# Half 1's tap rows accumulated in PSUM, parameters transposed by DMA, and a new instruction order, in a gated state-space and routed-expert kernel

## The chip, the cores and the metric

The kernel runs on one core of one Trainium2 chip, and all times are microseconds of that core. A core has five engines with queues of their own: PE (TensorE, matrix products), DVE (VectorE), ACT (ScalarE), POOL (GpSimd) and SP, which here issues loads and stores. Each engine takes the instructions of its queue in order, and waits for others through semaphores. The metric is the device time of one execution; of the kernel before, three executions took 186.1, 186.47 and 186.91 us, so the median is 186.47.

## The reference

The input `x` is one sequence of L = 2048 tokens with D = 512 channels, in bf16. The output mixes two branches with a gate for each token:

```
g = sigmoid((x * gate_w).sum(-1))
out = g * a + (1 - g) * b

a: K[d,l] = Re sum_n C[d,n] * dt[d]*B[d,n] * exp(dt[d]*A[d,n]*l)      (complex, n = 128 states)
   a      = causal convolution of x with K over l (through an FFT) + x * Dskip
b: r   = x @ w_r;  idx = the 2 tokens with the largest r
   y   = ((silu(x[idx] @ w_gate)) * (x[idx] @ w_up)) @ w_down * sigmoid(r[idx])
   b   = x, with y added at rows idx
```

`dt = exp(log_dt)`. The lags `l` are rounded to bf16 in the reference, so K takes the same value at many lags, and needs to be known only at a grid of lags.

## The kernel before, in words

Channels are split into two halves of 256 (`h` = 0, 1), tokens into two blocks of 1024 (`blk` = 0, 1). A helper class `Prog` records every operation with what it reads and writes, works out all waits from this, and emits each engine's queue. The order isn't found by a scheduler: the list `SEQ`, written out in the source, fixes it (a negative number puts an operation that could run on ACT or DVE on DVE). All operations go through helpers such as `TT` (a DVE product or sum), `AC` (an ACT function), `SCL` (a scaling on ACT or DVE), `EV` (an eviction of PSUM on ACT or DVE), so the profile gives the helper's line for them: L402 for `TT`, L414 for `AC`, L418 for `EV`, L422 for `SCL`, L425 for a load or store, L428 for an adding DMA of POOL.

The stages, which overlap:

1. **Parameters.** `A`, `B` and `C` are loaded as they lie, in rows of states, and turned by 24 TensorE transposes into PSUM (L545); `AL` (real part times dt) and `B16` (angles) come of them. `WW` holds the weights C·B·dt. `log_dt` comes on ACT's queue.
2. **Forward transform.** Each of eight jobs (block × frequency tile `ft`) multiplies the 1024 tokens with cosines and sines (`c_fwd`, tiles F0 to F3): eight matmuls per part give the sum of even and odd tokens (`plus`, L764), which is evicted into the spectrum `X`; four more with the doubled odd tokens subtracted (`minus`, L779) give the difference, evicted too. PSUM has three pairs of banks for this (`fw0`, `fw1`, `fw2`). Block 1 also takes spectra of block 0 as inputs.
3. **Routing.** u is also loaded transposed (`XT`, one transposing load of 2 MB on SP, L526) for the router's products; the top two rows are found, gathered, and sent through the FFN (WG, WU, WD). Their scaled result `ZB` is added into `xp`, a copy of x in device memory, by a scatter of POOL (L748); u is later reloaded from `xp` on SP.
4. **Tables of K.** `exps1`, `exps2`: 32 exponentials for the first lag grid (`TP`) and nine for the second (`EB`) for each half, on ACT. `trig`: angles scaled, a sine, a shift of the phase (L598), and a cosine. `tab1` and `tab2` multiply both on DVE. Slots 0 to 8 of the second table (`TQ`) are multiplied by the weights. The rows for slots 9 to 20 are these rows times a base factor (`BN`): for half 0 as four products, two of them kept apart in `EX` and summed in PSUM by the generation; for half 1 as a complex product with its sums on DVE (`cmul`).
5. **Generation of K** (`kgen`): 64 groups of matmuls (L810; L813 for `EX`) make K at the lag grid, in PSUM banks `kg0` to `kg3`, evicted as `KA`; a selection (`KC`, L827) follows.
6. **Spectrum of K** (`kspec`, L849): products of KC with the constant `c_ksp` give `KK`.
7. **Products** (`products`, DVE): complex products of X and KK, for each half and quarter of frequencies, with four sums per half on POOL's adding DMAs (`accum`, L428).
8. **Inverse** (`inverse`, L927; L930 for the edge correction `KX`·`CO`): eight PSUM banks; each is visited twice (`q` = 0, 1). The result times g goes into u by an adding DMA, or, for the last block, by a DVE instruction (L409). u has by then been multiplied by 1 − g (sixteen instructions, L977 on ACT and L978 on DVE). Stores go out on SP and ACT.

Some buffers share space: half 1's TP table with the FFN weights, c_inv (`G`) with part of it.

Of the kernel before, what the change touches and what calls it, by code (L numbers as in the profile page):

```python
# [247 lines left out]
ONPE = []  # L248
# [36 lines left out]
def kspec_mats():  # L285
# [35 lines left out]
    "73 20 18 0 1 2 3 5 4 24 6 23 27 69 51 70 60 47 54 61 53 65 58 59 52 68 28 29 30 45 50 62 49 64 66 57 43 74 41 79 46 67 77 31 -147 -146 -135 -136 -145 "  # L321
    "10 48 -138 13 11 25 -137 78 -148 81 63 76 19 21 22 71 75 12 26 -33 33 34 35 36 7 176 175 9 182 181 17 -175 37 42 -178 178 14 188 16 179 56 -184 184 "
    "185 44 138 -140 -142 142 148 -150 -152 140 143 -158 -157 -155 -156 55 72 187 80 15 84 82 -181 193 194 152 150 -165 -167 158 -160 -162 162 189 191 190 "
    "-168 8 85 90 91 86 87 -196 196 197 160 163 -225 -227 -228 92 93 94 95 96 113 97 165 168 -172 169 172 192 206 98 99 100 -102 186 200 201 225 228 231 "
    "229 38 102 103 104 105 198 213 230 232 242 321 -244 153 106 107 114 108 109 110 -200 244 245 248 246 247 -321 -319 251 207 40 83 39 111 112 118 130 "
    "131 115 116 170 -235 -234 173 235 236 202 204 250 -320 237 238 239 240 311 310 309 308 -120 120 124 121 125 299 203 205 383 249 -259 306 307 -209 209 "
    "241 303 304 305 253 252 254 255 256 259 263 302 301 -89 122 270 290 276 277 280 268 279 271 292 278 291 275 273 274 272 283 298 294 289 267 297 269 "
    "296 281 282 286 287 288 285 284 293 295 210 384 -212 300 218 219 -221 222 221 386 -124 126 127 132 212 89 257 260 265 262 264 261 266 348 352 350 312 "
    "-314 -316 -129 322 -326 326 323 324 -342 327 339 -339 -341 314 -332 -329 -331 -330 223 349 117 214 216 215 385 316 332 317 -336 -334 336 342 -346 346 "
    "343 344 -403 347 -404 -402 -401 334 392 394 337 393 391 395 -397 129 133 356 -358 404 -406 354 351 397 -412 -410 -411 355 406 358 398 388 399 389 407 "  # L330
    "408 -360 412 415 416 413 387 390 414 417 418 420 419 421 422 424 423 427 425 426 433 428 429 434 430 431 432 435 353 360 361 362 363 217 364 365 439 "
    "440 437 438 441 442 443 444 366 369 380 370 453 454 445 446 375 378 373 447 367 436 455 456 457 458 459 460 461 462 463 465 476 477 478 371 -382 449 "
    "474 473 475 -449 486 451 464 466 469 483 450 484 485 505 452 487 488 494 470 479 480 481 482 493 495 496 498 497 499 467 468 471 472 506 507 568 522 "
    "523 508 509 571 510 511 569 570 526 512 513 572 573 527 514 515 516 517 518 519 525 524 520 521 489 490 491 535 537 536 492 538 540 539 528 530 548 "
    "549 529 546 382 531 533 532 578 500 581 582 583 501 579 580 502 503 557 558 559 550 551 552 589 504 560 562 561 379 541 376 547 553 554 555 377 534 "
    "574 575 576 602 600 577 601 588 590 368 556 372 603 591 592 624 374 563 584 585 587 614 616 615 586 611 613 612 604 606 605 617 607 608 609 610 544 "
    "542 593 625 623 565 594 622 545 619 567 564 621 566 543 595 596 597 599 598 629 631 630 626 627 628 639 638 632 633 634 618 620 635 636 637 641 640 "
).split()]

KB = 1024  # L340


def bass_gated_mix__ssm_conv_s4__moe_arch_mod__prompt_kernel(nc, A_u, A_A_re, A_A_im, A_B_re, A_B_im, A_C_re, A_C_im, A_log_dt, A_Dskip,
# [22 lines left out]
    with ExitStack() as es:  # L366
# [190 lines left out]
        def cbc(c):  # L557
            return BP(0, 128, c, (0, 2), (1, D))
# [393 lines left out]
        def stage(n):  # L952
            P.stage = n
# [103 lines left out]
```

## Time and profile before

| what | us |
|---|---|
| median of three executions | 186.47 |
| the profiled execution's own time | 186.91 |
| its span (first to last event of the profile) | 185.1 |
| DVE busy | 154.6 (84%) |
| PE busy | 137.0 (74%) |
| ACT busy | 127.2 (69%) |
| POOL busy | 19.1 (10%) |
| first exponential starts | 9.28 |
| generation of half 1 starts on PE | 115.78 |
| last inverse matmul ends | 177.1 |

The profile is of one execution. Busy time is an average over stages with different limits, and the engines take turns in setting the pace, so the share alone doesn't say what a change is worth. PE's busy time counts overlapping matmuls at their modelled ends. An instruction that stands after another on the same engine can start a little before the end given for it, so steps are best counted from start to start. The granted clock of PE was 0.925 of full speed over the span.

### The profile page before, as it was taken

What the parts mean: (1) busy time and instruction counts of PE and PEld (TensorE: products, weight loads), DVE (VectorE), ACT (ScalarE), POOL (GpSimd) and SP (SyncE); (2) the same over time, 40 slices, a digit from 0 to 9 for tenths busy, and PEclk for the clock granted to TensorE, in tenths of its full rate; (3) what the DMA queues carried; (4) which work ended last, traced back from release to release, by engine and by line L of the source; (5) the groups of instructions that cost most, each with busy time, mean ns of one, the idle gap of its engine ahead of it and who ended that gap; (6) DMA issues with size and microseconds to landing.
All of it is one profiled execution on the core that took longest, in us unless ns stands there. A gap on an engine that the chain in (4) does not pass through costs nothing.

```text
span 185.1 us, 4226 instructions
## 1 busy us (share of the span) xinstructions
PE 137.0 (74%) x1806; PEld 93.5 (51%) x1806; DVE 154.6 (84%) x240; ACT 127.2 (69%) x226; POOL 19.1 (10%) x25
## 2 busy tenths in 40 slices
PE   0238999999999679987218781996632999999920
PEld 0133446444556223856205671964521788888810
DVE  0188699988999999999999999995299989999740
ACT  0399979999999999999975487392620067796100
POOL 3000000000000000000600000113000303066300
PEclk9999999999999969999657999699996599999996
DMA  4999999976509704004140830199950473859997
GB/s 76 314 214 283 247 255 378 411 251 255 202 9 345 273 4 113 4 4 117 35 125 2 307 150 0 32 204 343 240 100 0 80 147 64 166 57 149 152 215 225
DMA packets 28388, 30.28 MB, mean 164 GB/s; under 512 B 13479, under 2 KB 22962, under 8 KB 28210
## 3 DMA queue, kind: packets, MB, share of 16 engines
q1 hardware_dynamic: 21442, 23.36, 41.3%
q0 software_dynamic: 4352, 5.77, 19.5%
q10 hardware_dynamic: 2576, 0.89, 2.3%
q8 instruction: 14, 0.23, 0.5%
q14 instruction: 4, 0.03, 0.1%
HBM read 20.05 MB, written 4.20 MB: 131 GB/s over the span
## 4 chain that ended last, share of the span: by engine, by line
DVE 28%; ACT 28%; PE 22%; DMA 10%; SPq 4%; issue 3%; DVEq 0%
DVE AR L402 21%; PE ps L927 14%; ACT AR L414 13%; DMA AR<-AR 6%; ACT AR L602 5%; ACT AR L598 5%; PE ps L764 5%; SPq L425 4%; PE ps L849 3%; DMA AR<-c_fwd 3%; DVE AR L422 3%; ACT AR L422 2%; ACT AR L418 2%; DVE AR L409 1%; DVE AR L418 1%
## 5 line engine op out<-in xcount | busy, mean ns | idle before, releaser
L402 DVE TENSOR_TENSOR AR<-AR 128x1024 bf16<-128x1024 bf16 (+6 forms) x127 | 113.4, 930 | 8.6 <-DMA AR<-AR 5.2
L418 ACT ACTIVATE AR<-ps 128x1024 bf16<-128x1024 f32 (+3 forms) x40 | 32.3, 839 | 29.6 <-PE ps L849 20.2
L414 ACT ACTIVATE AR<-AR 128x256 bf16<-128x256 f32 (+3 forms) x100 | 40.7, 485 | 4.3 <-DVE AR L402 4.1
L927 PE MATMUL ps<-AR 128*128 128x256 bf16 x256 | 30.1, 277 | 8.1 <-DVE AR L402 8.1
L764 PE MATMUL ps<-AR 128*128 128x512 bf16 x128 | 30.9, 392 | 0.5 <-DMA AR<-c_fwd 0.5
L927 PEld LDWEIGHTS ps<-AR 128*128 128x128 bf16 x256 | 25.2, 99 | 11.8 <-DVE AR L402 5.8
L849 PE MATMUL ps<-AR 128*128 128x256 bf16 x160 | 20.5, 286 | 3.2 <-ACT AR L418 3.2
L428 POOL DMA_DIRECT2D AR<-AR x14 | 14.6, 1134 | 66.0 <-DVE AR L402 32.0
L764 PEld LDWEIGHTS ps<-AR 128*128 128x128 bf16 x128 | 12.7, 101 | 15.9 <-issue 2.3
L810 PE MATMUL ps<-AR 128*64 128x42 bf16 x512 | 15.0, 198 | 6.7 <-DVE AR L402 3.9
L849 PEld LDWEIGHTS ps<-AR 128*128 128x128 bf16 x160 | 16.0, 103 | 7.0 <-ACT AR L418 4.4
L779 PE MATMUL ps<-AR 128*128 128x512 bf16 x64 | 16.7, 398 | 2.8 <-DVE AR L418 2.8
L810 PEld LDWEIGHTS ps<-AR 128*64 128x64 bf16 x512 | 14.5, 124 | 8.0 <-DVE AR L402 4.1
L602 ACT ACTIVATE AR<-AR 128x1024 bf16<-128x1024 int16 (+1 forms) x14 | 14.8, 1067 | 1.3 <-DVE AR L598 1.1
L422 DVE TENSOR_SCALAR AR<-AR 128x256 int32<-128x256 f32 (+3 forms) x49 | 14.9, 346 | 0.8 <-ACT AR L602 0.7
L414 ACT ACTIVATE AR<-ps,AR 128x256 bf16<-128x256 f32 x24 | 10.0, 470 | 4.6 <-PE ps L927 4.4
L418 DVE CAST AR<-ps 128x1024 bf16<-128x1024 f32 (+2 forms) x10 | 10.6, 1073 | 2.1 <-PE ps L764 2.1
L827 PE MATMUL ps<-AR 128*32 128x128 bf16 (+1 forms) x96 | 7.5, 418 | 6.4 <-ACT AR L418 6.4
L779 PEld LDWEIGHTS ps<-AR 128*128 128x128 bf16 x64 | 6.1, 101 | 10.5 <-DVE AR L418 3.3
L748 POOL DMA_INDIRECT xp<-AR x1 | 2.3, 2319 | 87.6 <-DVE AR L406 87.6
L545 PE MATMUL ps<-AR 128*128 128x128 bf16 x24 | 2.9, 312 | 11.4 <-DMA AR<-in_A_A_re_dram 7.4
L977 ACT ACTIVATE AR<-AR 128x512 bf16<-128x512 bf16 x15 | 9.8, 717 | 0.0
(55 smaller groups left out, 111.7 us busy)
## 6 DMA issues: line engine op xcount, KB each, us to landing
AR<-AR POOLq DMA_DIRECT2D x8, 512.0 KB, 6.0
AR<-c_ksp SPq DMA_DIRECT2D x5, 512.0 KB, 4.4
AR<-in_A_u_dram SPq DMA_DIRECT2D x2, 1024.0 KB, 8.5
AR<-c_fwd SPq DMA_DIRECT2D x4, 512.0 KB, 5.6
AR<-xp SPq DMA_DIRECT2D x2, 1024.0 KB, 6.7
AR<-c_inv SPq DMA_DIRECT2D x1, 2048.0 KB, 12.2
AR<-in_B_w_gate_dram SPq DMA_DIRECT2D x1, 1792.0 KB, 11.9
AR<-in_B_w_up_dram SPq DMA_DIRECT2D x2, 896.0 KB, 12.2
```

What stands on the lines that cost most here:

```text
L402: return P.op(DVE, lambda h: h.tensor_tensor(out=o, in0=a, in1=b, op=op), rd, wr, cost=tt_cost(o, a, b), **k)
L414: return P.op(ACT, lambda h: h.activation(out=o, in_=a, func=func, scale=scale, bias=bias), rd, wr, cost=0.185 + nel(o) * 0.833e-3 + (0.09 ...
L418: return P.op((ACT, DVE), (lambda h: h.activation(out=o, in_=a, func=ACTF.Copy), lambda h: h.tensor_copy(o, a)), rd, wr, cost=(0.185 + n * ...
L422: return P.op((ACT, DVE), (lambda h: h.activation(out=o, in_=a, func=ACTF.Copy, scale=c), lambda h: h.tensor_scalar(out=o, in0=a, scalar1= ...
L428: P.op(POOL, lambda h: h.dma_start(o, i, accum_op=ALU.add), rd, wr, cost=1.4, nbytes=nbytes, dma=True, tag="sum")
L602: return x.activation(out=so(2), in_=lo, func=ACTF.Sin, scale=-SC16 if m else SC16, bias=HPI(0, 128, 0, (1, 1)) if m else 0.0)
L764: last = h.matmul(o, F[ft](0, 128, ((par * 4 + st) * 2 + part) * 128, (1, 128)), U(0, 128, (blk * 8 + st * 2 + par) * D, (1, D)), start=(i ...
L779: last = h.matmul(o, F[ft](0, 128, ((4 + st) * 2 + part) * 128, (1, 128)), UN(0, 128, st * D, (1, D)), start=False, stop=(st == 3 and blk ...
L810: last = hh.matmul(pb(64 * ct, 64, (g - b0) * 42, (1, 42)), TP[h][1 - part](0, 128, g * 128 + ct, (2, 64)), TQ[h][1 - part](0, 128, g * 84 ...
L849: last = hh.matmul(pb(0, 128, n * 256, (1, 256)), KPU[u](0, 128, tau * 128, (1, 128)), KC[h](0, 128, jg * 256, (1, 256)), start=(k == 0), ...
L927: last = hh.matmul(pb(0, 128, e * 256, (1, 256)), G(0, 128, ((par * 2 + part) * 4 + ft) * 512 + (2 * t2 + e) * 128, (1, 128)), X(0, 128, h ...
L977: P.op((ACT, DVE), (lambda h, o=o, tb=tb: h.activation(out=o, in_=o, func=ACTF.Copy, scale=SG(0, 128, 48 + tb, (1, 1))), lambda h, o=o, tb ...
```

## The change

The diff has these parts.

- Half 1's tap rows are made like half 0's: four products, two kept in `EX`, and 256 more matmuls in its generation sum them.
- The parameters come through six transposing loads on SP; the TensorE transposes and their copies go.
- u is no longer scaled by 1 − g. Each second visit of the inverse takes two more matmuls with the negative unit matrix, which subtract u in PSUM, and the edge correction moves from the first visit to the second.
- The forward transform has two PSUM pairs in place of three, and its jobs are listed in twos; generation has two banks in place of four; the selection uses the two banks of `misc`; in `kspec` the two parts of a block share one pair.
- Half 1's exponentials for the first grid are recorded beside half 0's; both halves use one `EB` buffer, as they did. The FFN weights WU and the intermediate CM1, CM2 and CMW move to the space of X, and KA of half 0 leaves the space of u.
- Some small copies of the routing are split or added.
- `SEQ` is another list throughout. In it the scaling of ZB stands after half 1's table on DVE (it stood before the tables' end), and with it the scatter and the reload of u; the first products of half 0 are followed by an eviction, two of KA, and CO; F2, F3 and the second half of u are loaded after XT.

```diff
 SEQ = [int(x) for x in (
...
-        CM1 = B("cm1", oG, 4 * KB, F32); CM2 = B("cm2", oG + 4 * KB, 4 * KB, F32); CMW = B("cmw", oG + 8 * KB, 4 * KB, F32)
+        CM1 = B("cm1", oB + 8 * KB, 4 * KB, F32); CM2 = B("cm2", oB + 12 * KB, 4 * KB, F32); CMW = B("cmw", oB + 24 * KB, 4 * KB, F32)
...
-        WU = [B("wu%d" % i, oF + (16 + 7 * i) * KB, 7 * KB) for i in range(2)]
+        WU = [B("wu%d" % i, oB + (8 + 16 * i) * KB, 7 * KB) for i in range(2)]
...
-        KA = [B("ka0", oA, 64 * 84), B("ka1", oE + 15 * KB, 64 * 84)]
+        KA = [B("ka0", oG + 16 * KB, 64 * 84), B("ka1", oE + 15 * KB, 64 * 84)]
...
-        fw2, pu = PB("fw2", 2, None), PB("pu", 3, None)
-        kgp = [PB("kg%d" % i, 2 + i // 2, i % 2) for i in range(4)]
+        kgp = [PB("kg%d" % i, 2, i) for i in range(2)]
...
-            DQ([(PRM(0, 128, i * D, (128, 4), (1, 128)), dr(prm[i], 0, (128, 128), (128 * 128, 4), (1, 128)))], [], [(PRM, i)], 131072)
+            dp[0] -= 1e3
+            P.op(SP, lambda h: h.dma_start_transpose(PRM(0, 128, i * D, (1, D)), dr(prm[i], 0, (128, D), (1, 128))), [], [(PRM, i)], cost=1.25, nbytes=200000, late=1.8, prio=dp[0])
...
-                        last = h.transpose(pt(0, 128, at + k * 128, (1, 128)), PRM(0, 128, i * D + k * 128, (1, 128)), CB(0, 128, 0, (1, 128)))
...
-        TT(f512(AL), f512(DTB), f512(PT0), ALU.mult, [DTB, (PT0.buf, 0)], [AL])
+        TT(f512(AL), f512(DTB), f512(PRM, 0), ALU.mult, [DTB, (PRM, 0)], [AL])
...
-        EV(BP(0, 128, 0, (1, 2 * D)), PT1(0, 128, 2 * D, (1, 2 * D)), [(PT1.buf, 4), (PT1.buf, 5)], [BP])
...
-            if h == 0:
-                SCL(nb(0, 128, 0, (1, 512)), bi(0, 128, 0, (1, 512)), -1.0, [bi], [nb])
+            SCL(nb(0, 128, 0, (1, 512)), bi(0, 128, 0, (1, 512)), -1.0, [bi], [nb])
             for j, s, c, m in ((13, 0, 8, 1), (9, 5, 4, 0)):
...
-                if h == 1:
-                    cmul(h, lambda p: sl(p, j, c), lambda p: sl(p, s, c), lambda p: bv((bi, br)[p]), ks, [bi, br], lambda p: [(tq(p), ("t", j))])
-                    continue
                 TT(sl(1, j, c), sl(1, s, c), bv(br), MUL, ka(1) + [br], [(qr, ("t", j))])
                 TT(sl(0, j, c), sl(0, s, c), bv(br), MUL, ka(0) + [br], [(qi, ("t", j))])
                 TT(xv(1), sl(0, s, c), bv(nb), MUL, ka(0) + [nb], [(EX[h][1], j)])
                 TT(xv(0), sl(1, s, c), bv(bi), MUL, ka(1) + [bi], [(EX[h][0], j)])
...
-                pb = (*fwp, fw2)[k % 3]
+                pb = fwp[k % 2]
...
-                pb = kgp[(b0 // 12) % 4]
+                pb = kgp[(b0 // 12) % 2]
...
-                                if h == 0:
-                                    last = hh.matmul(pb(64 * ct, 64, (g - b0) * 42 + 18, (1, 24)), TP[h][1 - part](0, 128, g * 128 + ct, (2, 64)),
+                                last = hh.matmul(pb(64 * ct, 64, (g - b0) * 42 + 18, (1, 24)), TP[h][1 - part](0, 128, g * 128 + ct, (2, 64)),
                                                  EX[h][1 - part](0, 128, g * 48 + ct, (2, 24)), start=False, stop=(part == 1), tile_position=(0, 64 * ct), skip_group_check=True)
...
-                pb = kgp[2 + bk % 2]
+                pb = misc()
...
+                    pb = fwp[i]
                     for part in range(2):
-                        pb = fwp[part]
...
-                                    if not q and t2 and e:
-                                        last = hh.matmul(pb(0, 128, 256, (1, HC)), KX(0, 128, (2 * blk + par) * 128, (1, 128)), CO[h](0, 128, 0, (1, HC)), start=False, stop=False)
+                                    if q:
+                                        last = hh.matmul(pb(0, 128, e * 256, (1, HC)), CB(0, 128, 768, (1, 128)), U(0, 128, (blk * 8 + (2 * t2 + e) * 2 + par) * D + h * HC, (1, HC)), start=False, stop=(e == 1 and not t2))
+                                    if q and t2 and e:
+                                        last = hh.matmul(pb(0, 128, 256, (1, HC)), KX(0, 128, (2 * blk + par) * 128, (1, 128)), CO[h](0, 128, 0, (1, HC)), start=False, stop=True)
...
+        exps1(1, (4, 4, 4, 4))
         stage("copy")
...
-        for tb in range(16):
-            o = U(0, 128, tb * D, (1, D))
-            P.op((ACT, DVE), (lambda h, o=o, tb=tb: h.activation(out=o, in_=o, func=ACTF.Copy, scale=SG(0, 128, 48 + tb, (1, 1))),
...
```

## The prediction

> **What bounds the kernel now.** I read the page's chain first: no engine owns the span, so the stages have to be taken one by one.
>
> ```profile
> DVE 28%; ACT 28%; PE 22%; DMA 10%; SPq 4%; issue 3%; DVEq 0%
> ```
>
> The timelines (start us, us, engine, line; in brackets the idle time before and what ended it) then give each engine's turns. First SP's queue, then PE:
>
> ```profile
> 12.02 12.32 SPq L526 DMA_TRANSPOSE AR<-in_A_u_dram  x1
> ```
>
> ```profile
> 7.40 1.03 PE L545 MATMUL ps<-AR 128*128 128x128 bf16 x8 [7.40 <-DMA AR<-in_A_A_re_dram]
> ```
>
> A_re lands at 7.4 and TensorE turns it. Its 2 MB sister, the transposing load of u, holds SP for 12.32 us. Next ACT at both ends of the table stage, and DVE after it:
>
> ```profile
> 9.28 11.44 ACT L414 ACTIVATE AR<-AR 128x256 bf16<-128x256 f32 x37 [3.10 <-DVE AR L402]
> ...
> 95.03 0.93 ACT L602 ACTIVATE AR<-AR 128x768 bf16<-128x768 int16 x1
> ```
>
> ```profile
> 96.00 18.55 DVE L402 TENSOR_TENSOR AR<-AR 128x256 bf16<-128x256 bf16 x19 [0.39 <-ACT AR L602]
> ...
> 132.87 8.93 DVE L402 TENSOR_TENSOR AR<-AR 128x1024 bf16<-128x1024 bf16 x11 [5.22 <-DMA AR<-AR]
> ```
>
> From 9.28 to the last cosine at 95.96, ACT is nearly full, with DVE beside it. Then DVE alone finishes half 1's table (weights, then tap rows), and only then PE starts half 1's kernel generation, at 115.78:
>
> ```profile
> 115.78 1.41 PE L810 MATMUL ps<-AR 128*64 128x42 bf16 x64 [3.86 <-DVE AR L402]
> ...
> 142.31 1.89 PE L927 MATMUL ps<-AR 128*128 128x256 bf16 x8 [5.57 <-DVE AR L402]
> ```
>
> DVE works through the products from 115.0 to 173.4. Its one long stall there, 5.22 us, waits for the second DMA addition on POOL's queue, as the chain says:
>
> ```profile
> 120.82 12.03 DMA AR<-AR
> ```
>
> It lands 12.0 us after issue while the 2 MB load of `c_inv` (issued 121.53, landed 12.2 later) moves; the first addition, issued 118.30 with little beside it, took 4.8. From 142.31 PE runs its inverse until 177.1, DVE ending just before; eight DVE closings and the last stores take the rest, to 185.1.
>
> **What the Trainium skill says.** "DMA: Bandwidth & Descriptors", section "Issuing engines are not separate DMA queues": loads from SP and POOL interleave on the same 16 DMA engines. The trace agrees (4.8 against 12.0 us). "TensorE: Matmul & The Clock Gate", Part 1: the clock halves after an idle window and returns after sustained work; here the granted clock was 0.5 from 142 to 146, after the 5.57 us wait. "VectorE: DVE Perf Modes", "Why PSUM operands drop a tier": PSUM reads are slower. A 1024-element copy from f32 PSUM took 1.22 us, a bf16 SBUF product of 1024 took 0.69.
>
> **The change, part by part.** Consecutive DVE instructions overlap, so I count start to start: products of 2304, 2048 and 1024 elements 1.39, 1.17 and 0.62; a 1024 PSUM copy 1.17 on DVE (0.95 on ACT); 512 columns 0.62.
>
> *Start.* Six plain loads, 24 TensorE transposes and one copy (`BP`) become six transposing loads on SP. The trace has only the 2 MB one. Each new one is 1/16 of its bytes: at least 12.32/16 = 0.77 us of SP. At most it also pays the 14.4 − 12.3 = 2.1 us by which that one landed after its issue: 2.9. A plain 128 KB load landed 5.1 after issue. A_re, now first at 0.73, lands between 0.73 + 0.77 + 5.1 = 6.6 and 8.7, against 7.4 + 1.03 of PE before. With 0.64 for `AL` the first exponential comes between 7.3 and 9.4, against 9.28. I take the middle: 1.1 us earlier. F2, F3 and the second half of u move behind u's 12 us transpose, so forward block 0 pauses for about 3 us near 26 to 29; ACT's exponentials, 0.306 each, and DVE's tables cover that. Without this cover the pause is the cost.
>
> *Tables, by engine.* Silu, Tanh, Sin and Exp still alternate in six table loads, so those cost nothing. Half 1's exponentials move ahead of the FFN loads' reuse of space: no work is added. "One shared buffer" changes nothing: both entries of `EB` are already `EB1`. Up to the last cosine, I counted the order on ACT: one more PSUM eviction (0.95) and two more phase shifts (1.25 each), +3.4. DVE gives up two shifts (0.6) and `BP` (0.7), and takes one KA and three KC evictions (0.6 each): +0.6, under ACT. The extra small routing copies, about 0.2 each, hide under the same span while both engines are not late. Last cosine: 95.96 − 1.1 + 3.4 = 98.3. Two forward PSUM pairs instead of three, and two kgen banks instead of four, tie PE to each eviction; I cost that at nothing: forward block 1's spectra are first read by the products after 115, so PE may run later there, and only generation of half 0, which the table's order gives 20 us before 96, must not. If that cover is gone it costs about 3 us (third rival).
>
> *Tap rows of half 1.* Six DVE products per group become four; the sums go to PSUM. Saved: 2 × 1.17 + 2 × 0.62 = 3.6. The negation goes to ACT, under the multiplies by the weights. `CO` (0.42) moves behind the products. DVE's tail, 115.78 − 95.96 = 19.8, becomes 15.8. Kernel generation of half 1 starts at T = 98.3 + 15.8 = 114.1: 1.7 earlier.
>
> *PE in generation.* 256 matmuls become 512. The same mix took 1.96 us per 96 in half 0 and 2.6 at 27 ns each. About 12 us instead of 6. Hidden in part by DVE's products of half 0, but ka1:12 and ka1:24 are now evicted on DVE behind five other instructions (ready T + 6.7 and T + 8.2), and c_inv waits for the last of it.
>
> *DVE after T, in its new order.* ZB scaling 0.27; four products 4.7; one KK eviction 1.17; KA 0.62, CO 0.43, KA 0.62; one product 1.17: T + 9.0, or 9.4 with the wait for kernel generation. Next is the result of the second addition, issued at T + 5.0. Before, four more products stood ahead of this wait. The scatter into `xp`, which was at 89.6, now waits for ZB at T; it takes POOL 2.32 us ahead of the first addition, whose input is ready only at T + 2.6, and lands 4.1 after issue. SP waits for that with c_inv and the stores queued behind, then issues the 2 MB reload of u at about T + 5. So the reload takes the place of c_inv beside that addition. Alone it would land at T + 10 to 11, with a share like c_inv's at T + 17. I take T + 16, a stall of 6.6 instead of 5.2. c_inv waits for generation (about T + 13) and lands near T + 24. Behind this stall are all second-quarter products, the KK1 eviction at T + 28, and CO of half 1 at T + 30.8, for which PE's third inverse job waits. The end of products: 57.7 us before, plus ZB, two KA, one KK, CO (0.27 + 1.24 + 1.17 + 0.42), minus one scaling 0.26, plus 1.4 of stall, minus 2.05 of smaller waits (0.46, 0.57, 0.27, 0.75) that I don't assume: T + 59.9.
>
> *PE's inverse.* The 16 scalings of u (15 on ACT, 9.8 us but off the path; one on DVE) go. In their place 32 matmuls of 256 columns subtract u in PSUM: 32 × 0.109 = 3.5. The eight edge matmuls move to the second visit. From CO on I follow the queue: five inverse and spectrum jobs to T + 36.6; then blocks of 42, 32 and again 42 and 32 matmuls, each 4.6 or 3.5 us, none short of its DVE input. The last ends at T + 66.1. Before it was 177.1 − 115.8 = 61.3: +4.8. What follows is unchanged, 8.0.
>
> **Sum.** Span 185.1 − 1.7 + 4.8 = 188.2. The profiled execution took 186.91, span plus 1.81; the median, 186.47, is 0.44 under that. So 188.2 + 1.37 = 189.6 us.
>
> **Rivals.**
> *Faster:* the addition isn't held up by the reload. It lands at T + 11, its 6 us typical; the stall falls from 6.6 to 1.6. PE's start is then set by c_inv at T + 24 to 26, so 4 of the 5 us are gained. With A_re at the early bound (−0.9): 184.7. For it: 4.8 to 6.1 us for additions without company. Against: 12.0, 10.2 and 11.6 beside a 2 MB load. It decides from a landing at about T + 12.
>
> *SP is clogged:* at 2.9 us each, six transposes take 17.4 us, u's transpose is issued at about 21, not 12, and F2, F3, router and FFN come 9 us later. Exponentials cover half: +5, 194.5. For it: SP's own 2.48 us pauses in the first 6 us. Against: 0.77 by bytes.
>
> *PSUM becomes the bound:* each of the later forward jobs and kgen banks waits for an eviction standing in ACT's or DVE's order. About eight waits of 0.4: +3, 192.6. For it: both engines are 9 tenths busy there. Against: in the trace PE waited 2.8 us for a forward eviction and no engine felt it.
>
> *It evens out:* the gained 3.6 us of taps and the start pay for everything: 186.5.
>
> **How the numbers follow.** Likeliest 0.43 (own range 187.4 to 192), faster 0.16, clogged 0.20, PSUM 0.14, even 0.07. About 0.5% (0.9 us) is what a measurement of this kernel can tell. Slower: 0.20 + 0.14 + 0.38 of the likeliest = 0.72. Same: 0.07 + 0.04 = 0.11; faster 0.17 with a remainder of the likeliest. Range 185.3 to 195.5: it takes in both ends of the start (−0.9, +1.2) and the clogged queue.
>
> **What would show it.** Right: first exponential near 8.2, generation of half 1 near 114, a DVE stall on a DMA addition near T + 9, twice as many kgen matmuls, PE's last inverse job about 8 us before the end. Wrong: first exponential after 10 or u's transpose issued after 16 (clogged); waits of PE on ACT or DVE evictions in forward that add up to over 4 us (PSUM); no DVE stall on the addition (faster); or ACT not being what ends the table stage at all.

## The result, and the profile after

The changed kernel takes 189.59 us (median of 4 runs, 188.88 to 193.0) against 186.44 before (4 runs, 186.1 to 186.91). The ratio is 1.0154, with a 95% interval of 1.0116 to 1.0193: 1.5% slower, with an interval clear of 1. The profiled execution took 189.57 us with a span of 187.8, against 186.91 and 185.1. Experiments 1 to 4 and 10 ran on one chip, 5 to 7 on a second, 8 and 9 on a third. On them the executions of the kernel before fall into two groups, 182.0 to 185.1 us and 185.3 to 188.4; its four executions above lie within the range of the upper one, so 1.0154 may understate the slowdown, and the ratios below leave the upper group out while the medians quoted do not.

The page's chain, which had no owner before, has one now:

```profile
PE 40%; ACT 21%; DVE 20%; DMA 10%; issue 4%; SPq 2%; DVEq 0%; ACTq 0%
```

The start, in the timelines of SP, ACT and PE (start us, us, engine and line; in brackets the idle time before and what ended it):

```profile
0.74 1.24 SPq L505 DMA_TRANSPOSE AR<-in_A_A_re_dram  x1
...
9.33 2.27 SPq L505 DMA_TRANSPOSE AR<-in_A_B_im_dram  x1
...
13.57 7.99 SPq L524 DMA_TRANSPOSE AR<-in_A_u_dram  x1
```

```profile
7.59 4.70 ACT L413 ACTIVATE AR<-AR 128x256 bf16<-128x256 f32 x15 [1.99 <-DVE AR L401]
...
99.74 0.93 ACT L588 ACTIVATE AR<-AR 128x768 bf16<-128x768 int16 x1
```

A small transposing load holds SP for 1.1 to 2.3 us, u's for 7.99. ACT starts 1.69 us earlier than before, yet its last cosine ends at 100.67, where it ended at 95.96. VectorE after that:

```profile
100.71 15.68 DVE L401 TENSOR_TENSOR AR<-AR 128x256 bf16<-128x256 bf16 x16 [0.96 <-ACT AR L588]
...
127.39 1.22 DVE L401 TENSOR_TENSOR AR<-AR 128x2048 bf16<-128x2048 bf16 x1 [3.32 <-DMA AR<-AR]
132.41 11.21 DVE L401 TENSOR_TENSOR AR<-AR 128x1024 bf16<-128x1024 bf16 x13 [3.80 <-DMA AR<-AR]
```

The tail of the tables, from the last cosine to the generation of half 1, is 15.8 us (19.8 before), so that generation starts at T = 116.45. The four products saved are real, but they only give back what the tables lost. Then VectorE waits twice, 7.1 us in all, for the two DMA additions of half 0. POOL's timeline says why those are late: the scatter, which was at 89.6 and took 2.32 us, now stands right ahead of them.

```profile
116.98 5.62 POOL L733 DMA_INDIRECT xp<-AR  x1 [27.83 <-DVE AR L405]
122.13 2.31 POOL L427 DMA_DIRECT2D AR<-AR  x2
```

On TensorE something new shows. In its timeline, between two matmuls of one accumulation group of the generation:

```profile
121.58 0.20 PE L799 MATMUL ps<-AR 128*64 128x24 bf16 x1 [0.98 <-issue]
...
127.09 0.18 PE L799 MATMUL ps<-AR 128*64 128x24 bf16 x1
131.24 0.20 PE L799 MATMUL ps<-AR 128*64 128x24 bf16 x1 [3.97 <-issue]
```

"issue" means that the engine waited for nothing the profile shows. There is no semaphore between the two instructions around the pause of 3.97 us. The table of windows of the same stretch (from:to, length, then busy us of PE, its weight loads, DVE, ACT, POOL; granted clock, DMA share, GB/s) shows how full the DMA engines are just then, with the two additions and the 2 MB reload of u (in the shorter pause, before 121.58, their share was 0.00):

```profile
124.00:126.00 2.00, 1.50 (x92) 1.41 (x87) 0.07 (x1) 0.53 (x1) 0.44 (x1) 1.00 1.04 197
126.00:128.00 2.00, 1.26 (x80) 1.17 (x74) 0.61 (x1) 0.65 (x2) 0.00 (x0) 1.00 1.08 175
128.00:130.00 2.00, 0.00 (x0) 0.00 (x0) 0.61 (x1) 0.00 (x0) 0.00 (x0) 1.00 1.06 207
```

The chain then runs through the late end of the generation, `c_inv`, and TensorE without a break to 182.8:

```profile
127.27 3.97 issue
...
131.66 10.95 DMA AR<-c_inv
142.66 1.89 PE ps L900 x8
```

So two paths leave T. One goes over the scatter and the additions to VectorE's products, which end at 177.51. The other goes over the generation and `c_inv` to TensorE's inverse. The experiments ask which of them sets the end, and which part of the change feeds it.

### The profile page after: what moved, and what is told of

It is laid out like the page before. It is cut to its first block, busy times and chain, and to the rows that moved or that the text cites. A ratio compares the mean times of both kernels' runs of the same rounds, so it can differ in the third digit from the quotient of the medians.

```text
span 187.8 us, 4736 instructions
## 1 busy us (share of the span) xinstructions
PE 147.7 (79%) x2070; PEld 101.2 (54%) x2070; DVE 153.0 (81%) x239; ACT 118.7 (63%) x211; POOL 22.4 (12%) x25
## 3 DMA queue, kind: packets, MB, share of 16 engines
q0 software_dynamic: 4352, 5.77, 19.8%
## 4 chain that ended last, share of the span: by engine, by line
PE 40%; ACT 21%; DVE 20%; DMA 10%; issue 4%; SPq 2%; DVEq 0%; ACTq 0%
PE ps L900 15%; DVE AR L401 15%; PE ps L749 9%; DMA AR<-c_inv 6%; ACT AR L588 6%; ACT AR L413 5%; DMA AR<-c_fwd 5%; ACT AR L584 4%; PE ps L764 4%; PE ps L835 4%; ACT AR L421 2%; ACT AR L417 2%; DVE AR L417 2%; DVE AR L421 2%; PE ps L903 2%
## 5 line engine op out<-in xcount | busy, mean ns | idle before, releaser
L401 DVE TENSOR_TENSOR AR<-AR 128x1024 bf16<-128x1024 bf16 (+8 forms) x127 | 113.3, 930 | 21.0 <-DMA AR<-AR 7.1
L417 ACT ACTIVATE AR<-ps 128x1024 bf16<-128x1024 f32 (+3 forms) x33 | 28.4, 879 | 38.0 <-PE ps L835 19.0
L749 PE MATMUL ps<-AR 128*128 128x512 bf16 x128 | 32.7, 411 | 13.2 <-DMA AR<-c_fwd 12.6
L413 ACT ACTIVATE AR<-AR 128x256 bf16<-128x256 f32 (+5 forms) x100 | 41.0, 486 | 3.0 <-DVE AR L401 2.0
L900 PE MATMUL ps<-AR 128*128 128x256 bf16 x256 | 33.3, 277 | 2.6 <-DMA AR<-c_inv 2.6
L835 PE MATMUL ps<-AR 128*128 128x256 bf16 x160 | 23.4, 311 | 7.3 <-ACT AR L417 6.3
L799 PE MATMUL ps<-AR 128*64 128x24 bf16 x512 | 19.2, 183 | 5.4 <-issue 5.4
L797 PE MATMUL ps<-AR 128*64 128x42 bf16 x512 | 19.2, 192 | 3.1 <-ACT AR L417 1.6
L799 PEld LDWEIGHTS ps<-AR 128*64 128x64 bf16 x512 | 18.5, 118 | 5.7 <-issue 5.7
L797 PEld LDWEIGHTS ps<-AR 128*64 128x64 bf16 x512 | 18.4, 117 | 4.4 <-ACT AR L417 1.7
L427 POOL DMA_DIRECT2D AR<-AR x14 | 15.2, 1268 | 39.9 <-DVE AR L401 31.1
L764 PE MATMUL ps<-AR 128*128 128x512 bf16 x64 | 17.3, 411 | 1.6 <-DVE AR L417 1.5
L417 DVE CAST AR<-ps 128x1024 bf16<-128x1024 f32 (+3 forms) x17 | 15.8, 943 | 1.5 <-PE ps L749 0.9
L584 ACT ACTIVATE AR<-AR 128x1024 int16<-128x1024 int16 (+1 forms) x9 | 11.7, 1302 | 0.3
```

Source lines behind the costliest of these rows:

```text
L401: return P.op(DVE, lambda h: h.tensor_tensor(out=o, in0=a, in1=b, op=op), rd, wr, cost=tt_cost(o, a, b), **k)
L413: return P.op(ACT, lambda h: h.activation(out=o, in_=a, func=func, scale=scale, bias=bias), rd, wr, cost=0.185 + nel(o) * 0.833e-3 + (0.09 ...
L417: return P.op((ACT, DVE), (lambda h: h.activation(out=o, in_=a, func=ACTF.Copy), lambda h: h.tensor_copy(o, a)), rd, wr, cost=(0.185 + n * ...
L584: q = P.op((ACT, DVE), (lambda x: x.activation(out=lo, in_=lo, func=ACTF.Abs), lambda x: x.tensor_scalar(out=w, in0=w, scalar1=16384.0, sc ...
L749: last = h.matmul(o, F[ft](0, 128, ((par * 4 + st) * 2 + part) * 128, (1, 128)), U(0, 128, (blk * 8 + st * 2 + par) * D, (1, D)), start=(i ...
L764: last = h.matmul(o, F[ft](0, 128, ((4 + st) * 2 + part) * 128, (1, 128)), UN(0, 128, st * D, (1, D)), start=False, stop=(st == 3 and blk ...
```

## The experiments

**1. The scatter early.** The changed kernel with the scaling of ZB, its two copies (now on VectorE) and the scatter moved ahead to about 90 us in the written order:

```diff
- "... -358 -160 355 ...   ... 416 147 148 160 164 117 ..."
+ "... -358 -160 -148 -149 160 164 355 ...   ... 416 117 ..."
```

> The changed kernel with one thing moved: the scaling of the expert's row, its two small copies and the scatter stand some 25 us earlier on VectorE and POOL, at about 90 us, so the 2 MB reload of u runs at about 95 us and is over when the generation of half 1 begins. Everything computed is the same. Theory A (full DMA engines hold up TensorE's instructions during the generation, and the end of the generation sets when c_inv is issued and so the end): the pause of 4.0 us inside the generation falls under 1, the generation ends near 127.5 in place of 131.7, c_inv lands near 135.5 in place of 142.6, the stalls of VectorE on the additions fall from 7.1 to 1 to 2 us, the last inverse matmul ends near 176 to 177, and the time is 183.5 to 185.6, 4 to 6 us under the changed kernel. Theory B (the amount of matmul work and VectorE's order set the end, the pauses are cover): the pauses may shorten, but the time falls by less than 2 us. Theory C (the earlier reload only moves the collision): a pause of 3 us or more shows in the forward transform or the tables at 90 to 105 us and the time stays within 1 us.

Measured: 184.59 us (20 runs, 183.41 to 187.16), 5.0 below the changed kernel (4.0 below its repeat in experiment 9); the kernel before, beside it, 186.46 (23 runs). Ratio to before 1.0047 [1.0002, 1.0092]. The time is theory A's; the mechanism isn't, as far as the one profile shows. That profile is of an execution of 187.07 us, 2.5 above the median. Its waits of PE and of DVE (us in all, times, longest):

```profile
PE ps L799 <- issue: 4.1, 2, 3.6
```

```profile
DVE AR L401 <- DMA AR<-AR: 1.2, 1, 1.2
```

The pause of TensorE stayed, and `c_inv` was issued at 132.85, not earlier. VectorE's wait on the additions fell from 7.1 to 1.2, a wait of 3.1 for TensorE's spectrum came in, and its products ended at 175.05, 2.5 earlier. The other path came down as much: `c_inv`, without the reload beside it, took 8.9 us to land in place of 10.95, and TensorE's run behind it was 1.5 us shorter, so the last matmul came at 180.40, 2.4 earlier. The price was the scatter's new place with the reload behind it, and by these profiles it was paid on both paths.

**2. No subtraction on TensorE.** The changed kernel without the 32 matmuls of `CB` by `U`:

```diff
-                                    if q:
-                                        last = hh.matmul(pb(0, 128, e * 256, (1, HC)), CB(0, 128, 768, (1, 128)), U(...), start=False, ...)
```

> The changed kernel without its 32 matmuls that subtract u in the last inverse visits; the output lacks the part of u that they take away, everything else stands. Theory A (from c_inv's landing the end is one unbroken run of TensorE work): the run from landing to last matmul shortens from 40.2 us by 32 x 0.109 = 3.5 at most, and by about 1.3 before VectorE's products limit it, time 188.3 (186 to 188.5). Theory B (VectorE's products set the end): the last matmul moves by less than 0.5 and the time by less than 0.5.

Measured: 188.91 us (4 runs), where the changed kernel gave 189.59 and, in experiment 9, 188.61. The last matmul ended 2.1 earlier (180.69) and the products at nearly the same place (177.35): the matmul is A's. The time lies between what the two theories asked for, and within the spread of the changed kernel's two medians; so by these runs the subtractions are worth about 1 us at most, not 3.5.

**3. The taps alone.** The kernel before, with half 1's tap rows as four products and 512 matmuls in its generation; nothing else:

```diff
-                if h == 1:
+                if False:
...
-                                if h == 0:
+                                if True:
                                     last = hh.matmul(pb(64 * ct, 64, (g - b0) * 42 + 18, (1, 24)), ...
```

> The kernel before with one part of the change alone: half 1 builds the tap rows of slots 13 to 20 as four products accumulated in PSUM, as half 0 does, and its generation takes both sets of matmuls; loads, buffers, scalings of u and the rest of the order stay. Theory A (the taps only shift work from VectorE to TensorE, and the DMAs behind them decide): VectorE reaches the generation about 3.6 us earlier (112.2 in place of 115.8), the generation grows from 5.6 to 9 to 11 us, its end and c_inv's issue fall within 1 us to 3 us later than before, the stall of VectorE on the addition falls from 5.2 to 1 to 3 us, and the time is 182 to 185. Theory B (the generation's end sets the end): c_inv is issued 1 to 3 us later than before, and the time is 186 to 189.

Measured: 186.9 us (6 runs) against 186.46; ratio 1.0134 [1.0046, 1.0223]. The time is theory B's. The generation took from 115.47 to 129.9, far more than expected; the pauses in it add up to 3.9 us, and `c_inv` was issued 8.4 later than before, not 1 to 3. T did not move, since the last cosine ended at 99.58 in place of 95.96: the first exponential came 0.8 later in this execution, and the negation stood on ACT ahead of the last cosine, where ACT waited 1.7 for VectorE. VectorE's long wait changed its name:

```profile
DVE AR L402 <- PE ps L813: 8.0, 1, 8.0
```

L813 is the generation's second set of matmuls. The wait on the addition (5.2) was gone.

**4. The transposing loads alone.** The kernel before, with the six parameters by `dma_start_transpose` and without TensorE's transposes and `BP`:

```diff
-            DQ([(PRM(0, 128, i * D, (128, 4), (1, 128)), dr(prm[i], 0, (128, 128), (128 * 128, 4), (1, 128)))], ...
+            P.op(SP, lambda h: h.dma_start_transpose(PRM(0, 128, i * D, (1, D)), dr(prm[i], 0, (128, D), (1, 128))), ...
```

> The kernel before with one part of the change alone: the six parameters by transposing loads on SP in place of straight loads, transposes on TensorE and the copy out of PSUM. Theory A (a transposing load of 128 KB holds SP for 1.24 us and lands about as early as the straight one did): first exponential at 7.4 to 7.8 in place of 9.28, the tables 1.5 us earlier, generation of half 1 at 114 to 115 in place of 115.8, time 185 to 186. Theory B (the start is given back at the next wait, on u's transposed load or the forward transform): first exponential as early, generation within 0.5 us of 115.8, time 186 to 187.

Measured: 189.79 us (4 runs), ratio 1.0325 [1.0219, 1.0431]; the generation began at 119.48. The first exponential came at 7.78, as both theories had it, and both missed the rest. PE's timeline shows one cost:

```profile
17.86 9.05 PE L753 MATMUL ps<-AR 128*128 128x512 bf16 x32 [17.86 <-DMA AR<-c_fwd]
```

In the old order of loads the six transposes push the forward constants back, and the forward transform starts at 17.86 (14.81 before). In the changed kernel it starts at 12.59, since the first u and `c_fwd` are issued third and fourth. So the new order of loads may be what the transposing loads need; no run has that order alone, and T came no earlier in the changed kernel either.

**5. The taps undone.** The changed kernel with the reverse of experiment 3's edit: 12 operations on VectorE, 256 matmuls.

> The changed kernel with the part of its title undone: half 1 builds the tap rows of slots 13 to 20 on VectorE (12 operations) and its generation is 256 matmuls again; all else as changed. Everything computed is the same. Theory A (the end of the generation and c_inv behind it set the end): VectorE reaches the generation 3.2 to 4 us later, at 119.6 to 120.4, the generation takes 5.7 without a pause and ends near 126, c_inv lands at 136 to 138 in place of 142.6, and the time is 183 to 187. Theory B (VectorE's order sets the end, as the prediction had it): the 3.6 us come back on VectorE's path, the reload and the scatter move with them, and the time is 190 to 193.

Measured: 195.81 us (4 runs), 6.2 above the changed kernel (7.2 above its repeat). Theory B, and more. T came at 119.50, about as expected, and the scatter, the reload and the additions moved with it. VectorE's timeline:

```profile
131.39 1.22 DVE L401 TENSOR_TENSOR AR<-AR 128x2048 bf16<-128x2048 bf16 x1 [4.27 <-DMA AR<-AR]
139.03 11.20 DVE L401 TENSOR_TENSOR AR<-AR 128x1024 bf16<-128x1024 bf16 x13 [6.41 <-DMA AR<-AR]
```

Now `c_inv` was issued at 129.24 and shared the DMA engines with reload and additions: it took 17.0 us to land, and the second addition ended VectorE's wait only at 139.03.

**6. The taps undone, with the scatter early.** The edits of experiments 1 and 5 together, which prices the title's part without the collision:

> The same undoing with the early scatter beside it, to be held against the early scatter alone (184.6 us): what the part of the title is worth when the reload is out of the way. Everything computed is the same. Theory A (with more matmuls the generation is held up by its instruction supply, so the part costs): generation ends at 125.5 to 126.5, c_inv lands at 134 to 136.5, time 181 to 184. Theory B (without the reload the part earns VectorE's 3.6 us): VectorE's products end 2 to 3.6 us later than with the early scatter alone, time 186 to 188.

Measured: 187.15 us (4 runs) against 184.59 in experiment 1. Theory B. The part of the title earns 2.6 us here by the medians, and 1.9% (3.4 us) by the two ratios to the kernel before (1.0234 and 1.0047), of the 3.6 it takes from VectorE. It isn't what made the kernel slower. (The two profiles have their products end within 0.2 us of each other, but that of experiment 1 is of an execution 2.5 above its median.)

**7. Two additions on VectorE, a miss.** A pair of DMA additions made by VectorE, in the changed kernel and in that of experiment 1:

```diff
-SUMS = ((0, 0), (0, 1), (1, 0), (1, 1))
+SUMS = ((0, 0), (0, 1), (1, 1))
```

> The changed kernel with the two additions of half 1's first products on VectorE (two additions of 128x2048, 1.18 us each in the trace) in place of two DMA additions of 512 KB; the 2 MB reload of u stays where it is. Everything computed is the same. Theory A1 (the packets of the DMA additions hold up TensorE's instructions): the pause of 4.0 us in the generation of half 1 falls under 1.5, the generation ends at 127.5 to 129 in place of 131.7, the time is 185 to 187.5. Theory A2 (the reload's packets hold them up): the pause stays at 3 us or more, the generation ends within 1 of 131.7, c_inv lands earlier by 1 to 2 at most since fewer bytes are under way, and the time is 187.5 to 190.

> The kernel with the early scatter, and also the two additions of half 1's first products on VectorE: no large transfer is under way while half 1 is generated. Everything computed is the same. Theory A (full DMA engines hold up TensorE's instructions): no pause over 1 us in the generation, it ends at 127 to 128.5, c_inv lands at 136 to 137.5, the last matmul is at 175 to 177 unless VectorE's 2.4 us more hold it, and the time is 180.5 to 184. Theory B (the pauses belong to TensorE's many short instructions, whatever the DMA engines do): pauses of 3 us in all remain, the generation ends at 131 or later, and the time is 184.5 or more.

Measured: 193.08 us and 187.5 us (4 runs each). I had taken the wrong pair: it starts at about 140, after the generation. Half 0's pair still ran inside it, and the pauses stayed (5.3 and 2.8 the longest). So neither run decides on the pauses. They do price VectorE at that place: 2.4 us more on it cost 2.9 over experiment 1. Over the changed kernel its cost can't be given closer than 1.6 to 4.5 us, since the four times of that run lie between 191.09 and 195.46.

**8. The right pair.** The kernel of experiment 1 with half 0's first pair on VectorE:

```diff
-SUMS = ((0, 0), (0, 1), (1, 0), (1, 1))
+SUMS = ((0, 1), (1, 0), (1, 1))
```

> The kernel with the early scatter, with the two DMA additions that VectorE's first products after the tap rows start (those of half 0, issued at 119.0 and 121.2 with the early scatter) made by VectorE. The two earlier runs of this kind had moved the pair of half 1, which starts after the generation. Everything computed is the same. Theory A (the packets of DMA additions hold up TensorE's instructions during the generation of half 1): no pause over 1 us in it, it ends at 127.5 to 129 in place of 132.9, c_inv lands at 136 to 138, and VectorE's 2.4 us more are taken from a wait on TensorE (3.1 us with the early scatter): time 182 to 184.5. Theory B (the pauses come with the many short matmuls whatever moves beside them): pauses of 2.5 us or more in all, the generation ends at 131 or later, and 2.4 us more on VectorE come out as 2 to 3: time 186 to 188.

Measured: 184.45 us (20 runs, 183.62 to 185.41); ratio to before 1.0058 [1.0029, 1.0088]. Theory A on the pauses: the waits of TensorE list no "issue" in the generation at all, though it ended at 130.3, later than A had it. The windows of the same table, at the same stage:

```profile
126.00:128.00 2.00, 2.00 (x82) 2.00 (x80) 1.97 (x3) 0.12 (x1) 0.00 (x0) 0.50 0.03 8
128.00:130.40 2.40, 2.31 (x123) 2.21 (x119) 2.33 (x5) 1.03 (x3) 0.00 (x0) 0.84 0.00 0
```

In these windows, with the DMA engines empty, the matmuls follow each other without a gap, and `c_inv` landed at 138.2. Every profile with 512 matmuls and additions in this stage has a pause of 2.8 us or more, up to 5.6. The granted clock is a rival: all but two of the 19 pauses in half 1's generation, over all profiles, begin at a clock of 1.0. Experiment 8 had that clock for only 5 us of its generation, with a wait of 1.6 us for an eviction in it, and experiment 10 for about 1 us. The kernels with 256 matmuls (before, experiments 4 to 6) have no pause there, but they too ran these matmuls mostly or wholly at half clock. The generation of half 0 shows what a full clock does alone, since it has 512 matmuls as well: in experiment 10 it ran at a clock of 1.00 and a DMA share of 0.13 without such a pause (with waits of 1.5 and 0.4 us for evictions in it), and the longest one there in any profile is 0.97 us. So the long pauses come with the transfers; a short one needs none.

The DMA packets suggest what TensorE lacks in a pause. The queue named "instruction" brings packets of 16 KB, 14 in the kernel before and 16 in the changed one. All those 19 pauses, in eight profiles, end 1.25 to 1.46 us after such a packet has ended; that of 3.97 us ends at 131.24, its packet at 129.85. In experiment 1 the pause lasts until 128.55, although the additions have landed by 126.78, since the packet comes only at 126.3 to 127.3. I read it as TensorE running out of instructions while their transfer stands behind the additions'. No run here moves the instruction transfer alone.

Yet the median did not move against experiment 1. VectorE was busy without a gap from 100.64 to 172.53, and that set the end. (This profile ends 2.5 us earlier than that of experiment 1, which is of a long execution; how long TensorE pauses there in a shorter one was not seen.)

```profile
142.51 30.01 DVE L401 TENSOR_TENSOR AR<-AR 128x2048 bf16<-128x2048 bf16 x36
```

**9. Three forward pairs in PSUM, and the changed kernel again.** The first has only its forward pool as before the change:

```diff
-                pb = fwp[k % 2]
+                pb = (*fwp, fw2)[k % 3]
```

> The changed kernel with three pairs of PSUM banks for the forward transform, as before the change, in place of two; the order of the instructions is left. Everything computed is the same. Theory A (the smaller pool costs next to nothing): TensorE's waits on evictions in the forward transform fall by 1 to 2 us, the last cosine of the tables moves by less than 0.7, time 188.8 to 190. Theory B (the rival of the prediction: PSUM is the bound): the tables end 1.5 us earlier or more, the generation of half 1 begins at 115 or earlier, time 185.5 to 188.

> The changed kernel itself once more, beside the two others on the same chip: 188.9 to 190.5, with a pause of 3 to 4 us in the generation of half 1 and c_inv landing at 141 to 144.

Measured: 192.76 us for the first (189.54 to 193.55) and 188.61 for the second (187.81 to 192.73, ratio 1.0156 [1.0001, 1.031]). The first run's time decides nothing, since the changed kernel itself takes 193 now and then, and its profile is of an execution of 193.55. But T is 117.26 in it, TensorE's waits on evictions in the forward transform are 4.4 us in place of 2.1, and ACT's on the forward matmuls 2.4 in place of 2.3: no sign that a larger pool brings the tables forward. That falls against PSUM as the bound. In this repeat the chain of the changed kernel takes the other path, the one that the prediction had followed:

```profile
117.03 5.62 POOL xp L733
122.64 0.13 POOL AR L427
122.77 8.70 DMA AR<-AR
```

The longest pause was 5.1 us here and `c_inv` was issued at 134.06, 2.4 later than in the first profile, and still VectorE's products (to 176.59) set the end. How near the two paths are can be estimated: where VectorE leads, the last matmul comes 4.97 us after the last product (the two runs of this experiment, and 5, 6 and 8). In the first profile that is 177.51 + 4.97 = 182.48, against 182.78 over `c_inv`. In the repeat `c_inv` gives 142.6 + 38.6 (TensorE's run after it in experiment 1) = 181.2, against 181.55 over the products. They lie within 0.4 us.

**10. Both paths cut.** Experiment 8 with four PSUM evictions moved from VectorE to ACT in the written order, and u scaled by 16 operations of ACT under the generation in place of the 32 matmuls:

```diff
-                                        last = hh.matmul(pb(0, 128, e * 256, (1, HC)), CB(0, 128, 768, (1, 128)), U(...), start=False, ...)
+        for tb in range(16):
...
+            P.op((ACT, DVE), (lambda h, o=o, tb=tb: h.activation(out=o, in_=o, func=ACTF.Copy, scale=SG(0, 128, 48 + tb, (1, 1))), ...
```

> The last kernel (early scatter, half 0's two additions on VectorE) with both long paths cut at once: the four evictions that VectorE still makes after the tap rows (0.6 to 1.2 us each, 3.7 in all) go to ScalarE, which is idle there, and u is scaled by 16 operations of ScalarE (0.63 us each) while half 1 is generated, in place of the 32 matmuls. Everything computed is the same. Theory A (VectorE's unbroken work from the tables on, and TensorE's from c_inv's landing on, end within 1 to 2 us of each other, so one alone earns little and both together earn most of it): VectorE's products end at 168 to 170 in place of 172.5, the last matmul at 173 to 175 in place of 178.4, the time is 180 to 182.5. Theory B (the stores and the additions of the outputs hold the end): the last matmul moves as in A, and the time stays at 183 to 185.

Measured: 183.83 us (22 runs, 182.68 to 184.53) beside 186.56 for the kernel before (27 runs, 182.58 to 188.0); ratio 1.000 [0.9963, 1.0038]. It is the fastest version here, 2.5 to 3% below the changed kernel. Against the kernel before its median is 2.7 us lower, but by the ratio the two are even, so it can't be said to beat it. Theory A's time missed, and theory B's cause isn't what the trace shows either. VectorE's 3.7 us turned into a wait:

```profile
139.59 2.36 DVE L401 TENSOR_TENSOR AR<-AR 128x2048 bf16<-128x2048 bf16 x2 [4.43 <-ACT AR L417]
...
142.44 30.02 DVE L401 TENSOR_TENSOR AR<-AR 128x2048 bf16<-128x2048 bf16 x36
```

L417 is the eviction of half 1's kernel spectrum, which needs the end of half 1's generation. VectorE's last 30 us start at 142.4 in both kernels, with or without the evictions. By this profile the floor of this order lies here: generation, spectrum, then 30 us of products.

The marks of all of these, from the profiles (us; pause is the longest "issue" in the generation, wait is VectorE's on DMA additions; the median is of all executions, and the profile of 1 is of one of 187.07 us):

| kernel | T | pause | `c_inv` lands | wait | products end | last matmul | median |
|---|---|---|---|---|---|---|---|
| before | 115.78 | none | 133.7 | 5.2 | 173.37 | 177.09 | 186.44 |
| changed | 116.45 | 4.0 | 142.6 | 7.1 | 177.51 | 182.78 | 189.59 |
| changed, again (9) | 116.49 | 5.1 | 142.6 | 5.9 | 176.59 | 181.55 | 188.61 |
| scatter early (1) | 116.45 | 3.6 | 141.8 | 1.2 | 175.05 | 180.40 | 184.59 |
| taps undone (5) | 119.50 | none | 146.2 | 10.7 | 184.13 | 189.09 | 195.81 |
| taps undone, scatter early (6) | 120.08 | none | 137.2 | 1.4 | 175.19 | 180.15 | 187.15 |
| right pair (8) | 116.37 | none | 138.2 | none | 172.53 | 177.49 | 184.45 |
| both paths cut (10) | 115.25 | none | 138.0 | none | 172.46 | 175.80 | 183.83 |

## Why the prediction was right, and where it was not

The time (189.6 against 189.59) and the span (188.2 against 187.8) agree, and the main mechanism was there: the scatter and the reload in front of the additions, and VectorE waiting for them. Three other terms were wrong and cancelled, so that the sum came this close is luck. (In the clogged rival, 189.6 + 5 is 194.6, not 194.5.)

*Start.* Taken at 8.2, measured 7.59: SP is held for 1.24 us by the first transposing load, inside the bounds of 0.77 to 2.9. SP was not clogged: u's transpose was issued at 13.57 and took 7.99, not 12.32, and the pause of about 3 us near 26 to 29 did not come. That rival is out for this order of loads; in the old one experiment 4 comes near it, with u's transpose issued at 15.24 and a time 3.3% over the kernel before.

*Tables: the step that failed.* "Last cosine: 95.96 − 1.1 + 3.4 = 98.3." It was 100.67. From the first exponential to the last cosine the windows of before and after (columns as above: ACT is the fourth busy time) are:

```profile
9.28:95.96 86.68, 71.21 (x1002) 39.46 (x1002) 80.32 (x151) 83.70 (x157) 3.05 (x3) 0.94 0.63 188
```

```profile
7.59:100.67 93.08, 80.18 (x1064) 44.73 (x1064) 80.09 (x151) 88.35 (x160) 0.56 (x2) 0.93 0.60 187
```

ACT was busy 88.35 us in place of 83.70, so +4.65 where I counted +3.4, with three instructions more (160 against 157), as counted; why their time grew by more stays open. Its idle time grew from 2.98 to 4.73, so +1.75 where I assumed none; 2.3 us of the idle time are waits on TensorE's forward matmuls:

```profile
ACT AR L417 <- PE ps L767: 1.9, 2, 1.2
...
ACT AR L417 <- PE ps L764: 0.4, 1, 0.4
```

The start gave 0.6 back. In experiment 9 a third PSUM pair left these waits as long (2.4), so the number of pairs is hardly their cause; the new order of the forward jobs may be, but no run isolates it, so that stays open.

*Tap rows.* VectorE's tail was 15.8, as predicted. "1.7 earlier" became 0.7 later, since all of it went to the tables. The 3.6 us are worth it all the same: undone, they cost 6.2 beside the scatter and the reload (experiment 5) and 2.6 without these (6).

*Generation.* Predicted about 12 us, measured 15.2. Without pauses it would have been about 9.7, at a clock of 1.0 throughout; the step left out that TensorE could pause with nothing to wait for: 5.4 us of pauses. `c_inv` landed at T + 26.2, not T + 24.

*The additions.* The step that carried the forecast holds: the scatter ahead of the additions, the reload beside them, a wait of 7.1 us (predicted 6.6) that ended at T + 16.0, to the tenth. Both additions were late and not only the second, and the scatter took 5.62 us, not 2.32. Moving it took 4.0 to 5.0 us off the time (experiment 1). The rival "faster" asked for a landing before T + 12, and the first addition alone did that. Products ended at T + 61.1 and, in the repeat, T + 60.1; predicted T + 59.9.

*TensorE's inverse.* "32 × 0.109 = 3.5" is a sum of work, not of time on the path. Where the path follows VectorE, the last matmul ends 4.97 us after the last product; with before's form of the inverse it is 3.7 (before, 3 and 4). The subtractions and the moved edges cost 1.25 there in place of 3.5, and without the subtractions the time moves by about 1 at most (experiment 2). The last inverse matmul came at T + 66.3 in the first profile, where TensorE's run hung on `c_inv`, 2.2 later than predicted, and at T + 65.1 in the repeat, where it followed VectorE; predicted was T + 66.1.

*What follows: "unchanged, 8.0".* It was 5.0. Before, the last stores waited for the last DMA addition of output rows: it was issued at 172.03 on POOL and landed at 178.94, and the stores on ACT's queue start at 178.97, well after TensorE's end at 177.09. In the changed kernel these stores start at 182.28, right behind the landing at 182.26: T + 65.8, where it was T + 63.2. Counted from there the span is 0.7 (T) + 2.6 − 0.6 (the stores) = 2.7 longer, as measured.

So the errors were +2.3 at T, +0.2 at the last matmul and −3.0 after it. The rival "PSUM becomes the bound" asked for over 4 us of TensorE's waits on evictions in the forward transform; there were 2.1, and in experiment 9 the larger pool brought T no earlier. The rival "evens out" needed the 3.6 us at T; they were gone by then.

## What to carry to other kernels

When work is moved off the engine that a path runs through, follow the next two paths to the same end before counting the gain: here VectorE's order, the chain through `c_inv`, and the spectrum of half 1 lie close together (the first two within 0.4 us), and each experiment that cut one of them earned less than it cut. A step that is moved carries its DMAs with it: the scatter of two rows, put next to two additions with the reload behind it, cost 4 to 5 us, more than any other part that was taken out of the changed kernel. And a tail taken over from before as "unchanged" has to be traced to what holds it, which may not be the engine that ends last.

## What the runs showed of the hardware

- Matmuls of one group can pause with no semaphore to wait for, when 512 short ones follow each other. With two DMA additions of 512 KB under way the longest pause of a generation was 2.8 to 5.6 us (eight profiles); with quiet DMA engines it was at most 0.98 (before 121.58 in the changed kernel, at a clock of 1.00). Each of the 19 pauses in half 1's generation ended 1.25 to 1.46 us after a packet of 16 KB of the queue "instruction".
- The same scatter of two rows took POOL 2.32 us at 89.6 us, and 1.53 at 91.7 in experiment 1, but 5.61 to 5.62 in every kernel that has it at T. What makes it longer there was not tried.
- The 2 MB transposing load of u held SP for 11.3 to 12.3 us in the old order of loads (before, experiments 3 and 4) and for 7.9 to 8.3 in the new; what makes the difference was not tried. As to loads that move together, the "DMA: Bandwidth & Descriptors" page of the Trainium skill, section "Issuing engines are not separate DMA queues", has the loads interleave on the same 16 engines, and the traces agree: the same `c_inv` load of 2 MB landed 7.6 us after issue in experiment 6, with the reload long over, and 17.0 beside the reload and the additions (experiment 5).
- TensorE's granted clock was 0.5 from 142.4 to 145.9 in the changed kernel, after a wait of 2.6 us for `c_inv`; in experiment 1, where TensorE hardly waited (0.6 us), it was 1.0 there, and the same run of work after `c_inv` took 38.6 in place of 40.1 us.
